# A mixed attention and gated-layer kernel: the products that feed the states are ordered after the scores instead of after the masking

## The chip, the cores and the metric

The kernel runs on one core of a Trainium2 chip. The metric is the device time in microseconds of one execution. The engines are TensorE (PE in the profile; PEld is its weight load), VectorE (DVE), ScalarE (ACT), GpSimd (POOL) and the DMA queues, which SyncE (SP) issues here.

## The reference

A gated linear attention runs over 768 tokens for each of 4 x 8 heads with 48 channels; its outputs for 3072 tokens then go through a gated layer of 384 x 1536 and back.

```python
for t in range(S):
    state = alpha[:, :, t, :, None] * state + np.einsum('bhd,bhe->bhde', k[:, :, t], v[:, :, t])
    y[:, :, t] = np.einsum('bhd,bhde->bhe', q[:, :, t], state)
...
gate = 1.0 / (1.0 + np.exp(-(x @ w_gate)))
val = x @ w_val
return (gate * val @ w_out).astype(np.float32)
```

## The kernel before, in words

**The gated layer.** The 3072 tokens form 6 groups of 512, and the layer's width of 1536 forms 12 blocks of 128, so there are 72 steps (`step`, L570). A step issues nine products of 128x512 into the PSUM bank `pg` (gate, through L208) and nine into `pv` (value). ACT takes the sigmoid of `pg` (`sg`, L581), DVE multiplies `pv` by it in place (L583), ACT rounds the result to `hh` (L585), and DVE writes the rest to `hl` (L586). The products back to 384 outputs (L594) are six with `hh` and three with `hl`. They are issued one step late: those of step s stand behind the gate and value products of step s+1. Each of `pg` and `pv` exists once, so the next `pv` product waits for L586 and the next `pg` product for the sigmoid, or for whatever else has read `pg`.

**The attention.** It is cut into 24 units, each a pair of heads times 512 tokens. Units 0 to 7 work in chunks of 128 tokens (`unit`, L398), units 8 to 23 in chunks of 64 (`late`, L481). In a late unit, in this order of data:

- DVE scales the queries (L501), scans the decays (L353, L355 to L357, L359) and leaves the keys to POOL (L360); PE turns the keys (L372) into `at_117`, and ACT copies them to `kn` (L376).
- PE computes the scores (L512): 16 products into columns 0 to 255 of two banks, `at_118` and `at_119` (`pas` in the code).
- DVE multiplies the scores by the mask into `A` (L517): four instructions, two for each bank.
- PE computes what the unit adds to the states, the "adds" (`adds`, L524, product L528): 16 small products into columns 256 to 447 of the same two banks.
- DVE steps the states through the unit (`states`, L536, L538): eight instructions in a chain, which read the adds out of the banks in turn. POOL multiplies the states by the decays (L543).
- One unit later, PE computes the outputs (L555) into `pg`, ACT and DVE move them to `yt` (L383, L384), and SP sends `yt` to `x` (L392), the gated layer's input of the next group.

Three steps of the gated layer go with each late unit.

**What sets the order.** Nothing is issued as it stands in the code. Each piece is handed to a planner (`Plan`, L45) with an engine, an assumed duration, a key (when it is due) and the names of what it reads and writes. `add` (L59) turns the names into dependences; `order` (L74) then plays the program through with the assumed durations: whenever an engine is free, the ready piece with the smallest key begins, and the pieces are issued in the order of these beginnings. The names are the planner's own: a name such as `at_118`'s stands for a whole bank unless a mark is added to it. The semaphores that the program really waits for are put in afterwards by the layer below, from the buffers that the issued instructions touch and from their order; it is not told of the planner's names.

In a late unit the keys are `A` (scores) = y + 0.50, `Y` (adds) = y + 0.51, `S` (states) = y + 0.55, `mask` = y + 0.6. So the adds are due ahead of the masks, but cannot begin in the plan until what they depend on is done.

Of the kernel before, what the change touches and what calls it, by code (L numbers as in the profile page):

```python
# [18 lines left out]
B, H, S, D = 4, 8, 768, 48  # L19
# [17 lines left out]
CH, EH = T // C, T // E  # L37
# [174 lines left out]
def chunked(ctx, tc, rows, vc, vh, weights_in, out, const, ident, flags, weights, within):  # L212
# [3 lines left out]
    plan = Plan()  # L216
# [12 lines left out]
    def borrow(tag, *shape):  # L229
        t, at = slots[tag]  # L230
        size = 1
        for x in shape:
            size *= x
        slots[tag][1] = at + size
        name = f"{tag}_{at}"
        held[tag].append(name)
        t = t[:, at:at + size]
        if len(shape) == 2:
            t = t.rearrange("p (a b) -> p a b", b=shape[1])
        elif len(shape) == 3:  # L240
            t = t.rearrange("p (a b c) -> p a b c", b=shape[1], c=shape[2])
        return name, t
# [17 lines left out]
    for _ in range(2):  # L260
        nm, t = borrow("w11", WF // 2, 2)
# [84 lines left out]
    def decays(u, size, t, inn, tin):  # L346

        n, nch = T, T // size
        a0, az, kT = tin[:, 0:nch], tin[:, A_Z:A_K], tin[:, A_K:A_Q]
        over = ["later"] if size == E else []  # L350
        (gn, G), (fn, F), (g0n, G0), (decn, dec) = r_G.next(), r_F.next(), r_G0.next(), r_dec.next()
        G0, dec = G0[:, 0:nch], dec[:, 0:nch]
        plan.add("vector", scan(n), t["G"], lambda: nc.vector.tensor_tensor_scan(  # L353
            out=G[:, ::-1], data0=az[:, n:0:-1], data1=d1g[size], initial=0.0, op0=ALU.mult, op1=ALU.add), [(inn, "a"), *over], [gn], port=True)
        plan.add("vector", 0.12, t["G"], lambda: nc.vector.tensor_tensor(out=G0, in0=G[:, 0:n:size], in1=tiny[:, 0:nch], op=ALU.max), [gn], [g0n], port=True)  # L355
        plan.add("vector", 0.12, t["G"], lambda: nc.vector.reciprocal(out=d1f[:, 0:n:size], in_=G0), [g0n], ["d1f"])
        plan.add("vector", scan(n), t["G"] + 0.01, lambda: nc.vector.tensor_tensor_scan(  # L357
            out=F, data0=az[:, 0:n], data1=d1f, initial=0.0, op0=ALU.mult, op1=ALU.add), ["d1f", (inn, "a")], [fn], port=True)
        plan.add("vector", 0.12, t["dec"], lambda: nc.vector.tensor_tensor(out=dec, in0=a0, in1=G[:, 0:n:size], op=ALU.mult), [gn, (inn, "a")], [decn], port=True)  # L359
        plan.add("gpsimd", pool_(n), t["kt"], lambda: nc.gpsimd.tensor_tensor(out=kT, in0=kT, in1=G, op=ALU.mult), [gn, (inn, "r")], [(inn, "k")])  # L360
        plan.add("gpsimd", 0.15, t["flag"], lambda: nc.gpsimd.tensor_copy(out=starts[:, u, 0:nch], in_=G[:, 0:n:size]), [gn], [("start", u)])
        return fn, F, decn, dec
# [5 lines left out]
    def turn(t, inn, kT, pkn, pk):  # L368

        def turned():  # L370
            for c in range(CH):
                nc.tensor.transpose(out=pk[:, c * P:(c + 1) * P], in_=kT[:, c * P:(c + 1) * P], identity=ident)  # L372

        plan.add("tensor", (0.109 * CH + 0.03, 0.9), t["X"], turned, [(inn, "k")], [pkn])
        knn, kn = r_kn.next()
        plan.add("scalar", act(CH * P), t["kn"], lambda: nc.scalar.copy(  # L376
            out=kn.rearrange("p c d -> p (c d)"), in_=pk[:, 0:CH * P]), [pkn], [knn])
        return knn, kn
# [102 lines left out]
    def late(u, g, p, t):  # L481
# [17 lines left out]
        fn, F, decn, dec = decays(u, E, t, inn, tin)  # L499
# [5 lines left out]
        knn, kn = turn(t, inn, kT, pkn, pk)  # L505
# [22 lines left out]
                    nc.tensor.matmul(out=pas[c % 2][1][R * j:R * j + D, T // 2 + c // 2 * D:T // 2 + (c // 2 + 1) * D],  # L528
                                     lhsT=kn[ro, c // 2, R * j:R * j + D], rhs=v[ro, c // 2, j], start=True, stop=True)

        plan.add("tensor", (0.045 * EH + 0.1, 0.5), t["Y"], adds, [knn, (vn, "v")], [x[0] for x in pas])
        st, sn = sts[p], ("st", p)
        done = EH if u >= EARLY + NP else CH
        plan.add("gpsimd", 0.28, t["G"], lambda: nc.gpsimd.tensor_copy(out=st[:, 0, :], in_=st[:, done, :]), writes=[sn])
# [3 lines left out]
                nc.vector.scalar_tensor_tensor(out=st[:, c + 1, :], in0=st[:, c, :], scalar=dec[:, c:c + 1],  # L538
                                               in1=pas[c % 2][1][:, T // 2 + c // 2 * D:T // 2 + (c // 2 + 1) * D], op0=ALU.mult, op1=ALU.add)

        plan.add("vector", 0.265 * EH, t["S"], states, [decn, *(x[0] for x in pas)], [sn])
        for j in range(2):
            plan.add("gpsimd", pool_(EH * D), t["sd"], lambda j=j: nc.gpsimd.tensor_tensor(  # L543
                out=vs[own[j], j], in0=st[own[j], 0:EH], in1=dec[own[j]].rearrange("p (c o) -> p c o", o=1).broadcast_to([R, EH, D]), op=ALU.mult),
# [74 lines left out]
    def begin(u):  # L619
        g, p = divmod(u, NP)  # L620
        if g == 0:
            z = 2.0 * p - 60.0
            t = dict(load=z - 5, G=z, dec=z + 0.5, kt=z, flag=14.0 + u, q=z + 0.2, X=z, kn=z, Y=z + 0.1, A=z, mask=z + 0.3,
                     S=z + 0.2, sd=z + 0.3, out=z + 0.4, y=z + 0.4, run=1, e_q="gpsimd")
        elif g == 1:
            z = 2.0 + 2.5 * p
            t = dict(load=z - 7, G=z, dec=z + 0.5, kt=z, flag=14.0 + u, q=z + 0.2, X=z, kn=z, Y=z + 0.1, A=z, mask=z + 0.3,
                     S=z + 0.2, sd=z + 0.3, out=last_step(u) + 0.52, y=z + 0.4, run=1, e_q="gpsimd")
        else:
            o = last_step(u)  # L630
            y = o - 3
            t = dict(load=y - 5, G=y - 2.9, dec=y - 2, kt=y - 2.7, flag=y + 1 + 0.5 * p, q=y - 2.0, X=y - 0.50, A=y + 0.50, kn=y - 1,
                     Y=y + 0.51, mask=y + 0.6, S=y + 0.55, sd=y + 0.7, out=o + 0.52, y=o - 99, run=100, e_q="vector")
        return unit(u, g, p, t) if u < EARLY else late(u, g, p, t)
# [13 lines left out]
    for s in range(NG * NF):  # L648
        step(s)
        if s in finished:  # L650
# [7 lines left out]
    every, one, total = sb.tile([P, 1], F32, name="every"), sb.tile([P, 1], F32, name="one"), r_at.next()  # L658
    nc.vector.memset(one, 1.0)
    late, n_units = NG * NF - 4, NG * NP  # L660
    plan.add("scalar", 0.5, late, lambda: nc.scalar.activation(out=starts.rearrange("p u c -> p (u c)"), in_=starts.rearrange("p u c -> p (u c)"),
                                                               func=AF.Abs, accum_out=flags[:, n_units:n_units + 1]),
             [("start", x) for x in range(n_units)], [("flag", n_units)])
# [152 lines left out]
```

## Time and profile before

| what | value |
|---|---|
| device time, 3 runs | 577.41, 577.44, 579.86 us (median 577.44) |
| device time of the profiled execution | 577.62 us |
| its span in the trace | 575.9 us |
| mean granted TensorE clock | 0.988 |
| busy: PE, PEld, DVE, ACT, POOL | 554.9, 438.5, 361.8, 184.1, 101.6 us |

The span runs from the first to the last instruction of the program; 1.7 us of the device time lie around it. Times below are microseconds from the start of the span. A row of the timeline gives start, length, engine, line, operation, what it writes and reads with their shapes, the count of merged instructions, and in brackets the idle time of the engine ahead of it with the releaser. The records of PE overlap, since its products are pipelined: what a run of products costs is the distance from its start to the start of the next run.

### The profile page before, as it was taken

The numbers are of one execution on the slowest core, as the hardware profiler recorded it, in microseconds if no ns is written. First come the engines' busy times: TensorE is split into PE (matmuls) and PEld (weight loads), VectorE is DVE, ScalarE is ACT, GpSimd is POOL, SyncE is SP. The second block draws the span as 40 slices with busy tenths as digits, with TensorE's granted clock in tenths as the row PEclk, the third lists the DMA queues.
The fourth block names the chain that finished last, engine by engine and source line by source line (L and its number), as shares of the span: only waits on it lengthen the run. The fifth ranks groups of instructions, "written<-read, shape, count | busy, mean of one in ns | idle before, by whom it ended". The sixth has DMA issues, their size and how long they took to land.

```text
span 575.9 us, 10284 instructions
## 1 busy us (share of the span) xinstructions
PE 554.9 (96%) x4150; PEld 438.5 (76%) x4150; DVE 361.8 (63%) x648; ACT 184.1 (32%) x331; POOL 101.6 (18%) x133
## 2 busy tenths in 40 slices
PE   7978799999999999999999999999999999999995
PEld 4566577787887887887887887888887888888784
DVE  7898999987586586585586586585595342321221
ACT  2568685532322222321222322222322221212111
POOL 5432220323021121121121121120120010000000
PEclk9979899999999999999999999999999999999998
DMA  8866656524234034134034143033132011100001
GB/s 319 265 222 211 224 169 209 163 71 126 75 90 113 8 103 111 62 106 110 3 111 110 56 111 100 11 112 96 70 111 53 9 28 28 56 0 0 2 1 61
DMA packets 21834, 55.93 MB, mean 97 GB/s; under 512 B 3473, under 2 KB 8593, under 8 KB 21777
## 3 DMA queue, kind: packets, MB, share of 16 engines
q1 hardware_dynamic: 21776, 55.17, 31.5%
q8 instruction: 35, 0.57, 0.4%
q14 instruction: 23, 0.18, 0.1%
HBM read 41.01 MB, written 4.72 MB: 79 GB/s over the span
## 4 chain that ended last, share of the span: by engine, by line
PE 88%; DVE 5%; DMA 3%; ACT 2%; POOL 1%; issue 1%; SPq 0%; DVEq 0%
PE po L594 27%; PE pg L208 25%; PE pv L208 25%; PE pg L555 3%; DMA first_w<-in_w_dram 2%; PE at L528 2%; PE at L512 2%; PE at L372 1%; PE at L424 1%; DVE first_w L323 1%; DVE w L327 1%; DMA x<-yt 1%; PE pg L475 1%; PE pg L471 1%; DVE raw L323 1%
## 5 line engine op out<-in xcount | busy, mean ns | idle before, releaser
L208 PE MATMUL pg<-x,w 128*128 128x512 f32 x648 | 164.7, 398 | 6.8 <-DMA x<-yt 2.5
L208 PE MATMUL pv<-x,w 128*128 128x512 f32 x648 | 160.0, 391 | 0.0
L583 DVE TENSOR_TENSOR pv<-pv,sg 128x512 f32<-128x512 f32 x72 | 50.3, 699 | 160.4 <-PE pv L208 159.3
L208 PEld LDWEIGHTS pg<-x,w 128*128 128x128 f32 x648 | 122.9, 191 | 36.7 <-DMA x<-yt 2.7
L208 PEld LDWEIGHTS pv<-x,w 128*128 128x128 f32 x648 | 121.2, 188 | 26.2 <-DVE hl L586 0.4
L594 PE MATMUL po<-hh,w 128*128 128x512 f32 x432 | 117.0, 404 | 0.0
L581 ACT ACTIVATE sg<-pg 128x512 f32<-128x512 f32 x72 | 43.0, 597 | 206.4 <-PE pg L208 206.3
L594 PEld LDWEIGHTS po<-hh,w 128*128 128x128 f32 x432 | 78.4, 188 | 18.0 <-issue 0.6
L543 POOL TENSOR_TENSOR vs<-st,dec 64x384 f32<-64x384 f32 x32 | 31.2, 974 | 239.8 <-DVE st L538 238.6
L585 ACT CAST hh<-pv 128x512 fp32r<-128x512 f32 x72 | 42.4, 588 | 80.2 <-DVE pv L583 80.2
L586 DVE TENSOR_TENSOR hl<-pv,hh 128x512 fp32r<-128x512 f32 x72 | 49.4, 686 | 24.3 <-ACT hh L585 23.7
L594 PE MATMUL po<-hl,w 128*128 128x512 f32 x216 | 64.0, 403 | 0.0
L594 PEld LDWEIGHTS po<-hl,w 128*128 128x128 f32 x216 | 39.5, 188 | 9.5
L360 POOL TENSOR_TENSOR in<-in,G 128x512 f32<-128x512 f32 x22 | 29.8, 1356 | 67.6 <-DVE G L353 38.7
L501 DVE TENSOR_TENSOR A<-A,F 64x512 f32<-64x512 f32 x32 | 37.4, 1170 | 0.9 <-DMA A<-in_rows_dram 0.4
L538 DVE SCALAR_TENSOR_TENSOR st<-st,dec,at 128x48 f32<-128x48 f32 x128 | 33.7, 264 | 5.3 <-PE at L528 0.3
L353 DVE TENSOR_TENSOR_SCAN G<-in,d1g 128x512 f32<-128x512 f32 x22 | 26.8, 1220 | 2.7 <-DMA in<-in_rows_dram 2.2
L357 DVE TENSOR_TENSOR_SCAN F<-in,d1f 128x512 f32<-128x512 f32 x22 | 27.9, 1266 | 0.5
L517 DVE TENSOR_TENSOR A<-at,mask 64x256 f32<-64x256 f32 x64 | 27.0, 422 | 1.1
L376 ACT COPY kn<-at 128x512 f32<-128x512 f32 x22 | 12.9, 585 | 34.5 <-PE at L372 34.5
L365 ACT ACTIVATE F<-F 128x512 f32<-128x512 f32 x23 | 14.5, 632 | 24.1 <-DVE A L501 20.0
L323 DVE SCALAR_TENSOR_TENSOR raw<-raw 128x576 uint32<-128x576 uint32 (+1 forms) x28 | 21.2, 765 | 0.5 <-ACT raw L320 0.5
(132 smaller groups left out, 413.9 us busy)
## 6 DMA issues: line engine op xcount, KB each, us to landing
in<-in_rows_dram SPq DMA_DIRECT2D x16, 516.5 KB, 4.1
raw<-in_w_dram SPq DMA_DIRECT2D x12, 576.0 KB, 4.6
x<-yt SPq DMA_DIRECT2D x35, 192.0 KB, 3.7
first_w<-in_w_dram SPq DMA_DIRECT2D x10, 576.0 KB, 5.4
out_dram<-raw SPq DMA_DIRECT2D x18, 256.0 KB, 2.4
v<-in_vc_dram SPq DMA_DIRECT2D x22, 192.0 KB, 3.5
A<-in_rows_dram SPq DMA_DIRECT2D x32, 128.0 KB, 3.9
in<-in_rows_dram SPq DMA_DIRECT2D x4, 772.5 KB, 7.1
```

The source lines that it names most:

```text
L208: nc.tensor.matmul(out=dst, lhsT=lhs(a, i), rhs=rhs(b, i), start=(n == 0 and i == 0), stop=(n == len(todo) - 1 and i == NK - 1))
L323: plan.add("vector", 0.07 + n / 860, kk, lambda upper=upper, lower=lower, a=a, x=x, y=y: nc.vector.scalar_tensor_tensor(out=lower, in0=upp ...
L357: plan.add("vector", scan(n), t["G"] + 0.01, lambda: nc.vector.tensor_tensor_scan(out=F, data0=az[:, 0:n], data1=d1f, initial=0.0, op0=ALU ...
L360: plan.add("gpsimd", pool_(n), t["kt"], lambda: nc.gpsimd.tensor_tensor(out=kT, in0=kT, in1=G, op=ALU.mult), [gn, (inn, "r")], [(inn, "k")])
L501: plan.add("vector", vec(T), t["q"], lambda j=j: nc.vector.tensor_tensor(out=A[own[j], j], in0=A[own[j], j], in1=F[own[j]], op=ALU.mult), ...
L538: nc.vector.scalar_tensor_tensor(out=st[:, c + 1, :], in0=st[:, c, :], scalar=dec[:, c:c + 1], in1=pas[c % 2][1][:, T // 2 + c // 2 * D:T ...
L543: plan.add("gpsimd", pool_(EH * D), t["sd"], lambda j=j: nc.gpsimd.tensor_tensor(out=vs[own[j], j], in0=st[own[j], 0:EH], in1=dec[own[j]]. ...
L581: plan.add("scalar", act(T), s - 100, lambda: nc.scalar.activation(out=sg, in_=got["g"][1][:, 0:T], func=AF.Sigmoid), [got["g"][0]], [sgn])
L583: plan.add("vector", vec(T), s - 100, lambda: nc.vector.tensor_tensor(out=pv, in0=pv, in1=sg, op=ALU.mult), [sgn], [pvn])
L585: plan.add("scalar", act(T), s - 100, lambda: nc.scalar.copy(out=hh, in_=pv), [pvn], [hhn])
L586: plan.add("vector", vec(T), s - 100, lambda: nc.vector.tensor_tensor(out=hl, in0=pv, in1=hh, op=ALU.subtract), [pvn, hhn], [hln])
L594: nc.tensor.matmul(out=pso_now[m][1][:, 0:T], lhsT=weights.part("o", b, f)[:, m * P:(m + 1) * P], rhs=h[a][:, 0:T], start=(f == 0 and i == ...
```

## The change

The planner's names for the adds and the states in `late` are changed; no instruction is added, removed or resized.

```diff
-        plan.add("tensor", (0.045 * EH + 0.1, 0.5), t["Y"], adds, [knn, (vn, "v")], [x[0] for x in pas])
+        plan.add("tensor", (0.045 * EH + 0.1, 0.5), t["Y"], adds, [knn, (vn, "v"), *(x[0] for x in pas)], [(x[0], "d") for x in pas])
...
-        plan.add("vector", 0.265 * EH, t["S"], states, [decn, *(x[0] for x in pas)], [sn])
+        plan.add("vector", 0.265 * EH, t["S"], states, [decn, *((x[0], "d") for x in pas)], [sn])
```

Before, the adds wrote the two banks, so in the plan they came after every earlier reader of the banks, the four masks. Now they read the banks, which makes them follow the scores alone, and write a part of its own, `"d"`, which the states read. The masks still read the bank's name.

TensorE at a late unit, before. `pg_120` is the outputs' and the gate's bank, `po` the three banks of the products back, `at_118` and `at_119` those of the scores and adds, `x_111` the layer's input; in brackets are the engines whose semaphores a row waits for.

```order
L555 MATMUL pg_120<-A_87,vs_89 48x64 x14
L594 MATMUL po_122<-hh_114,w_544 128x512 x2
L528 MATMUL at_118<-v_80,kn_84 48x48 [waits DMAHW1_49,DVE_49]
L528 MATMUL at_118<-v_80,kn_84 48x48
L528 MATMUL at_119<-v_80,kn_84 48x48 [waits DVE_49]
L594 MATMUL po_122<-hl_116,w_544 128x512
L208 MATMUL pg_120<-x_111,w_647 128x512 [waits DVE_49]
L208 MATMUL pg_120<-x_111,w_647 128x512 x8
L208 MATMUL pv_121<-x_111,w_647 128x512 x9
```

The same unit now; rows that differ from these by the bank alone are left out in both.

```order
L555 MATMUL pg_120<-A_87,vs_89 48x64 x14
L528 MATMUL at_118<-v_80,kn_84 48x48 [waits DMAHW7_49,DVE_49]
L528 MATMUL at_118<-v_80,kn_84 48x48
L528 MATMUL at_119<-v_80,kn_84 48x48 x2
L594 MATMUL po_122<-hh_114,w_544 128x512 x2
L594 MATMUL po_122<-hl_116,w_544 128x512
L208 MATMUL pv_121<-x_111,w_647 128x512 [waits DVE_49]
L208 MATMUL pv_121<-x_111,w_647 128x512 x8
L208 MATMUL pg_120<-x_111,w_647 128x512 [waits DVE_49]
L208 MATMUL pg_120<-x_111,w_647 128x512 x8
```

The adds moved from between the `hh` and the `hl` products to right behind the outputs, ahead of the `hh` products; they kept one wait for DVE and lost the second; and in the step that follows, the value products changed places with the gate products.

VectorE at a late unit, before. The rows L517 are the masks, L538 the first of eight state steps.

```order
L517 TENSOR_TENSOR A_87<-at_118,mask_104 64x4x64 [waits PE_49]
L517 TENSOR_TENSOR A_87<-at_119,mask_104 64x4x64 [waits PE_49]
L517 TENSOR_TENSOR A_87<-at_118,mask_104 64x4x64
L586 TENSOR_TENSOR hl_116<-pv_121,hh_114 128x512 [waits Activation_49]
L517 TENSOR_TENSOR A_87<-at_119,mask_104 64x4x64
L384 TENSOR_TENSOR yt_85<-pg_120,yt_85 128x512 [waits DMAHW6_49,DMAHW7_49,DMAHW5_49,Activation_49]
L538 SCALAR_TENSOR_TENSOR st_110<-st_110,dec_99,at_118 128x48 [waits PE_49]
L501 TENSOR_TENSOR A_86<-A_86,F_92 64x512 [waits DMAHW2_49]
L583 TENSOR_TENSOR pv_121<-pv_121,sg_112 128x512 [waits PE_49,Activation_49]
L353 SCALAR_TENSOR_TENSOR G_90<-in_78,d1g_102 128x512 [waits DMAHW0_49,Pool_49]
L586 TENSOR_TENSOR hl_116<-pv_121,hh_114 128x512 [waits Activation_49]
L355 TENSOR_TENSOR G_94<-G_90,tiny 128x8 [waits DVE_49]
```

The same unit now, from the third mask on.

```order
L517 TENSOR_TENSOR A_87<-at_118,mask_104 64x4x64
L586 TENSOR_TENSOR hl_116<-pv_121,hh_114 128x512 [waits Activation_49]
L538 SCALAR_TENSOR_TENSOR st_110<-st_110,dec_99,at_118 128x48 [waits PE_49]
L384 TENSOR_TENSOR yt_85<-pg_120,yt_85 128x512 [waits DMAHW6_49,DMAHW7_49,DMAHW0_49,Activation_49]
L517 TENSOR_TENSOR A_87<-at_119,mask_104 64x4x64
L501 TENSOR_TENSOR A_86<-A_86,F_92 64x512 [waits DMAHW2_49]
L353 SCALAR_TENSOR_TENSOR G_91<-in_79,d1g_102 128x512 [waits DMAHW1_49,Pool_49]
L355 TENSOR_TENSOR G_95<-G_91,tiny 128x8 [waits DVE_49]
L583 TENSOR_TENSOR pv_121<-pv_121,sg_112 128x512 [waits Activation_49]
L356 RECIPROCAL d1f<-G_95 128x8 [waits DVE_49]
L357 SCALAR_TENSOR_TENSOR F_93<-in_79,d1f 128x512 [waits DVE_49]
L586 TENSOR_TENSOR hl_115<-pv_121,hh_113 128x512 [waits Activation_49]
```

The states moved ahead of `yt` and of the fourth mask; the first three masks stay ahead of them; and the product L583 with the gate, and the L586 behind it, moved behind the scans of the decays.

This holds for units 9 to 23. In unit 8, the first late one, both masks of `at_119` come after the states, and the adds, which stood behind a later gate product before, stand behind the outputs too. Up to there the order is as before. PE also issues the turn of the keys (L372) of units 10 to 22 ahead of the value products of that step, where it stood behind them, and for units 10 to 20 two of the six `hh` products with it. In the queue of SP the load of `v` (L493) now comes ahead of the unit's transfers of `yt` to `x` (L392), not behind or among them.

## The prediction

> **What bounds the kernel now.** I read the busy time of each engine by windows first, then the timelines of PE and DVE over one late unit.
>
> ```profile
> 120.00:150.00 30.00, 30.00 (x243) 24.15 (x242) 23.31 (x46) 8.58 (x18) 7.99 (x10) 1.00 0.28 78
> 250.00:300.00 50.00, 50.00 (x391) 40.28 (x390) 34.57 (x61) 12.74 (x25) 11.05 (x14) 1.00 0.25 69
> 500.00:540.00 40.00, 40.00 (x175) 32.59 (x174) 8.65 (x13) 7.70 (x13) 0.00 (x0) 1.00 0.03 12
> ```
>
> ```profile
> 132.87 0.69 PE L512 MATMUL at<-A,in 48*64 48x64 f32 x32
> ```
>
> The columns of the first are the window, its length, then PE, PEld, DVE, ACT and POOL busy, and the granted clock. From 120 us on PE is busy in every microsecond, at a clock of 1.00, and every late unit lies there: the first one's scores, the second fence, begin at 132.87. So PE's own queue sets the time: a microsecond in which PE stands still is a microsecond on the end, and only what shortens PE's sequence gains anything. DVE, the next, is busy for 34.57 of 50.
>
> ```profile
> 242.67 0.69 PE L512 MATMUL at<-A,in 48*64 48x64 f32 x32
> 243.30 1.10 PE L555 MATMUL pg<-A,vs 128*48 128x64 f32 x32
> 244.33 1.67 PE L594 MATMUL po<-hh,w 128*128 128x512 f32 x6
> 245.93 0.72 PE L528 MATMUL at<-v,kn 64*48 64x48 f32 x32
> 246.58 0.96 PE L594 MATMUL po<-hl,w 128*128 128x512 f32 x3
> 247.38 2.24 PE L208 MATMUL pg<-x,w 128*128 128x512 f32 x9
> 249.46 2.20 PE L208 MATMUL pv<-x,w 128*128 128x512 f32 x9
> 251.50 1.57 PE L594 MATMUL po<-hh,w 128*128 128x512 f32 x6
> 252.91 0.87 PE L594 MATMUL po<-hl,w 128*128 128x512 f32 x3
> 253.62 2.24 PE L208 MATMUL pg<-x,w 128*128 128x512 f32 x9
> 255.69 2.21 PE L208 MATMUL pv<-x,w 128*128 128x512 f32 x9
> 257.74 0.60 PE L372 MATMUL at<-ident,in 128*128 128x128 f32 x4
> 258.10 1.65 PE L594 MATMUL po<-hh,w 128*128 128x512 f32 x6
> 259.58 0.86 PE L594 MATMUL po<-hl,w 128*128 128x512 f32 x3
> ...
> 264.49 0.69 PE L512 MATMUL at<-A,in 48*64 48x64 f32 x32
> ```
>
> One late unit on PE takes 264.49 - 242.67 = 21.82 us, from start to start without a gap. The stretch that the change rearranges runs from the end of the outputs (244.33) to the next step's products (247.38): `hh` 1.60, adds 0.65, `hl` 0.80, together 3.05 us.
>
> ```profile
> 242.85 0.70 DVE L583 TENSOR_TENSOR pv<-pv,sg 128x512 f32<-128x512 f32 x1 [3.73 <-PE pv L208]
> 243.58 1.29 DVE L517 TENSOR_TENSOR A<-at,mask 64x256 f32<-64x256 f32 x3
> 244.90 0.69 DVE L586 TENSOR_TENSOR hl<-pv,hh 128x512 fp32r<-128x512 f32 x1
> 245.60 0.42 DVE L517 TENSOR_TENSOR A<-at,mask 64x256 f32<-64x256 f32 x1
> 246.06 0.69 DVE L384 TENSOR_TENSOR yt<-pg,yt 128x512 fp32r<-128x512 f32 x1
> 246.67 2.42 DVE L538 SCALAR_TENSOR_TENSOR st<-st,dec,at 128x48 f32<-128x48 f32 x8
> 249.01 2.54 DVE L501 TENSOR_TENSOR A<-A,F 64x512 f32<-64x512 f32 x2
> ...
> 252.50 1.23 DVE L353 TENSOR_TENSOR_SCAN G<-in,d1g 128x512 f32<-128x512 f32 x1
> ...
> 255.44 1.23 DVE L357 TENSOR_TENSOR_SCAN F<-in,d1f 128x512 f32<-128x512 f32 x1
> ```
>
> The masks cannot begin at the scores' end (243.30), since the product L583 stands ahead of them and waits for `pv`: they begin at 243.58, the third ends at 243.58 + 1.29 = 244.87, the fourth at 246.02. PE pays little for this now: the adds begin at 245.93, after 1.60 us of `hh` products that cover the masks.
>
> **The wait that stays.** The change frees the adds from the masks in the plan alone. In the order the adds' first row still waits for DVE. Its bank, `at_118`, is read by the first and the third mask; the second wait, for the fourth mask, is gone because that mask now stands behind the states. So the adds wait for the third mask, and what covered it, the `hh` products, now stands behind them. Queued behind the waiting adds are all products of the gated layer.
>
> The Trainium skill's page "PSUM — Partial Sum Buffer", section "PSUM bank collisions raise a hardware error", says that two engines on one bank and 32-partition quadrant at once are an error even at disjoint columns, and that the guard goes by bank and quadrant. By that rule the masks and the adds exclude each other whatever the planner's names say. The order agrees, since the wait is there; no run here shows a collision.
>
> How long PE stands, from the delay between DVE's end and PE's start, and what the adds cost where nothing holds them:
>
> ```profile
> 66.21 0.68 DVE L384 TENSOR_TENSOR yt<-pg,yt 128x512 fp32r<-128x512 f32 x1
> ...
> 66.95 0.78 PE L208 MATMUL pg<-x,w 128*128 128x512 f32 x1 [2.43 <-DVE yt L384]
> ```
>
> ```profile
> 137.59 2.23 PE L208 MATMUL pg<-x,w 128*128 128x512 f32 x9
> 139.75 0.57 PE L528 MATMUL at<-v,kn 64*48 64x48 f32 x32
> 140.25 2.34 PE L208 MATMUL pv<-x,w 128*128 128x512 f32 x9
> 142.43 0.86 PE L594 MATMUL po<-hh,w 128*128 128x512 f32 x3
> ```
>
> - Added: PE starts 66.95 - 66.89 = 0.06 us after DVE ends, so the adds begin at 244.87 + 0.06 = 244.93 instead of 244.33: 0.60 us of standing in each unit.
> - Adds: in unit 8 they take 140.25 - 139.75 = 0.50, against 0.65 in later units, where the fourth mask (to 246.02) ends only after they have begun. That wait goes. I take 0.50; the upper end is 0.65.
> - Removed: changes between large and small products. `hh` products behind small ones and ahead of large ones take 259.58 - 258.10 = 1.48, `hl` behind `hh` take 253.62 - 252.91 = 0.71, against 1.60 and 0.80.
>
> New stretch: 0.60 + 0.50 + 1.48 + 0.71 = 3.29 us against 3.05, so +0.24 us a unit, in units 9 to 23: 15 x 0.24 = 3.6 us. With 0.65 for the adds it is 0.39, 5.9 us in all.
>
> Unit 8 is different: there only two masks, not three, stand ahead of the adds, so I expect no standing. Its adds leave the middle of the gate and value products, which now take 2.16 and 2.18 where elsewhere they take 2.08 (247.38 to 249.46) and 2.04 (249.46 to 251.50): -0.2 us.
>
> The value products swapped with the gate products, and the turn ahead of them, are the same products; I cost them at nothing, if what they wait for comes in time. In times of the unit above, PE then has: adds 244.93, `hh` 245.43, `hl` 246.91, value 247.62, gate 249.66, `hh` 251.74, `hl` 253.15, gate 253.86, turn 255.93 (0.36), two `hh` from 256.29, value at about 256.84. The waits to check:
> - The gate products at 249.66 wait for `yt` (L384), now behind the states. The states begin when DVE is free of L586 (245.59) and end at 248.02; `yt` ends at 248.72. Margin 0.9.
> - The value products at 256.84 wait for L586 of the step before, now behind both scans. The fourth mask ends at 249.15, L501 at 251.70, L353 at 252.95, then L355, L583, L357 and L586 (0.16, 0.70, 1.23, 0.69), with 0.4 for a reciprocal and gaps: 256.1. Margin 0.7.
> - `yt` is 248.72 - 246.75 = 2.0 us later, and so is `x`, which the next group needs after units 11, 15 and 19:
>
> ```profile
> 225.21 1.18 SPq L392 DMA_DIRECT2D x<-yt  x2
> ...
> 231.80 1.55 PE L208 MATMUL pg<-x,w 128*128 128x512 f32 x6
> ```
>
> ```profile
> x<-yt SPq DMA_DIRECT2D x35, 192.0 KB, 3.7
> ```
>
> The second transfer begins at 225.8 and lands by about 229.5, 2.3 us ahead of the products. The products come 0.2 later, so 0.5 is left. A landing slower by 0.8 would cost 0.3 three times, 1 us.
>
> Sum: 3.6 - 0.2 = +3.4 us on the profiled execution's 577.62 us, 581.0. The median of the runs, 577.44, is 0.2 lower, so I predict **580.8 us**, 0.6% slower. A measurement of this kernel can tell about 0.5%, 2.9 us, from no change.
>
> **The rivals.**
>
> *The wait is as harmless as the diff says* (faster). If the third mask ended before 244.33, PE would go straight on from the outputs: 0.50 + 1.48 + 0.71 = 2.69 against 3.05, -0.36 a unit, 15 x -0.36 - 0.2 = -5.6, 571.8 us. It decides at one point: whether the third mask is 0.6 us earlier. Against it: L583, which the masks stand behind, still waits for `pv`, as the 3.73 us of idle time ahead of it show. Chance 0.06.
>
> *Standing and saving cancel* (577.4). For this the standing has to be 0.36, a third mask 0.24 earlier, or the saving larger. Half of the saving is a sum of small distances, and +3.4 is only 0.5 above what can be told, so 0.22 for all that ends within 0.5%.
>
> *A second wait, at the value products.* DVE now does L355 between the scan and the product with the gate, and POOL's work on the keys starts with the end of the same scan.
>
> ```profile
> L501 DVE TENSOR_TENSOR A<-A,F x32: 661/1215/1303, 124.8 to 446.7; 64x512 f32<-64x512 f32 x32
> ```
>
> ```profile
> L355 DVE TENSOR_TENSOR G<-G,tiny x18: 152/943/1046, 95.2 to 428.7; 128x8 f32<-128x8 f32 x16, 128x4 f32<-128x4 f32 x2
> ```
>
> ```profile
> 253.86 1.28 POOL L360 TENSOR_TENSOR in<-in,G 128x512 f32<-128x512 f32 x1 [2.23 <-issue]
> ```
>
> Both rows (shortest, median and longest in ns) show two lengths, and the long one is met where POOL runs, as at L360. If POOL is first after the scan, L355 ends 1.4 us after 252.95 instead of 0.2, L586 ends at 257.3, and the value products wait 0.5 us, in units 9 to 22: 14 x 0.5 = 7, 588 us. Against it: POOL began 0.13 us after the scan's end (253.73), and L355 follows on DVE's own queue; L501 may also be the short one. The Trainium skill's page "SBUF — State Buffer", section "Who interferes with whom", says that a DVE instruction with two SBUF inputs contends with GpSimd's reads and that issue order decides who blocks. By that rule DVE, the earlier, would win and this rival fall; the two lengths agree with the rule. Chance 0.13.
>
> **How the numbers follow.** The forecast with its own range (580.3 to 583.2, the adds at 0.65) has 0.54, and 0.05 goes to late `x` on top of it (about 582); with the second wait (0.13) slower is 0.72. Within 0.5% is 0.22, faster 0.06. Leaving out the faster case and the second wait leaves out 0.19, so the range runs from 577.2 to 583.6.
>
> **What would show it.** In the profile after: PE idle or waiting for DVE L517 ahead of L528, some 0.5 to 0.6 us in 15 units; L528 straight behind L555, with `hh` products 0.5 after it; a unit of 22.06 us instead of 21.82; PE below 100% in windows from 150 us. Wrong would be: no wait there (faster), a wait at `pv` for L586 (slower than my range), or a unit of 21.82.

## The result, and the profile after

| | before | after |
|---|---|---|
| median of the runs, first set | 579.58 us (577.41 to 580.42, 6 runs) | 583.33 us (582.45 to 585.26, 6 runs) |
| median of the runs, second set | 579.38 us (577.14 to 580.52, 11 runs) | 582.94 us (581.84 to 584.52, 6 runs) |
| profiled execution: time, span | 577.62, 575.9 us | 582.92, 580.9 us |
| DVE busy in it | 361.8 us | 341.8 us |
| start to start of two late units | 21.82 us | 22.11 us |

The changed kernel is slower: ratio 1.0077, 95% interval [1.006, 1.0095], and 1.0072 [1.005, 1.0093] in the second set. The ratios follow the means of the runs more than the medians: the means are 579.05 and 583.46 us in the first set (+4.4) and 578.93 and 583.01 in the second (+4.1). The median of 583.33 is 2.5 us above the predicted 580.8. It lies inside the range of 577.2 to 583.6 and 0.1 above the forecast's own range of 580.3 to 583.2; the sections below show where the 2.5 us come from.

PE's wait after the change, from the list of waits (engine, line, the engine waited for; us in total, times, longest):

```profile
PE at L528 <- DVE A L517: 7.9, 15, 0.5
```

The row is new, fifteen waits of 0.5 us, the adds for the third mask, and from 100 us on it is the only one that the list has. The list counts from the modelled end of the last product ahead; from run to run of products, as below, PE stands a little longer.

The late unit that the prediction used, on PE after the change (start, us, engine, line; in brackets the idle time ahead and its releaser):

```profile
244.33 0.69 PE L512 MATMUL at<-A,in 48*64 48x64 f32 x32
244.95 1.10 PE L555 MATMUL pg<-A,vs 128*48 128x64 f32 x32
246.58 0.57 PE L528 MATMUL at<-v,kn 64*48 64x48 f32 x32 [0.53 <-DVE A L517]
247.08 1.67 PE L594 MATMUL po<-hh,w 128*128 128x512 f32 x6
248.59 0.86 PE L594 MATMUL po<-hl,w 128*128 128x512 f32 x3
249.29 2.24 PE L208 MATMUL pv<-x,w 128*128 128x512 f32 x9
251.37 2.20 PE L208 MATMUL pg<-x,w 128*128 128x512 f32 x9
...
257.61 0.60 PE L372 MATMUL at<-ident,in 128*128 128x128 f32 x4
...
258.51 2.23 PE L208 MATMUL pv<-x,w 128*128 128x512 f32 x9
...
...
262.23 2.24 PE L208 MATMUL pg<-x,w 128*128 128x512 f32 x9
...
266.44 0.69 PE L512 MATMUL at<-A,in 48*64 48x64 f32 x32
```

And DVE's part of it:

```profile
245.24 1.29 DVE L517 TENSOR_TENSOR A<-at,mask 64x256 f32<-64x256 f32 x3
...
249.54 0.68 DVE L384 TENSOR_TENSOR yt<-pg,yt 128x512 fp32r<-128x512 f32 x1
```

The outputs take 1.03 us (before: 243.30 to 244.33), so they end at 244.95 + 1.03 = 245.98. The third mask ends at 245.24 + 1.29 = 246.53 and the adds begin at 246.58: PE stands 0.60. Then adds 0.50, `hh` 1.51 and `hl` 0.70, and the step's products begin at 249.29. From 245.98 that is 3.31 us, against 3.05 before. The unit takes 266.44 - 244.33 = 22.11, which is 0.29 more, so 0.26 of it are in this stretch.

Where the two executions part, by the starts of the scores in unit 8 (before: 132.87, in the prediction), unit 9 and unit 23. Before:

```profile
155.41 0.69 PE L512 MATMUL at<-A,in 48*64 48x64 f32 x32
460.82 0.69 PE L512 MATMUL at<-A,in 48*64 48x64 f32 x32
```

After:

```profile
133.57 0.69 PE L512 MATMUL at<-A,in 48*64 48x64 f32 x32
155.88 0.69 PE L512 MATMUL at<-A,in 48*64 48x64 f32 x32
465.43 0.70 PE L512 MATMUL at<-A,in 48*64 48x64 f32 x32
```

Unit 8 takes 22.31 instead of 22.54 (-0.23). The fourteen units 9 to 22 take 309.55 instead of 305.41 (+4.14, 0.296 each). Ahead of unit 8 lie +0.70, where the order is the same in both. With about 0.25 in unit 23, which has the stretch but no turn of keys behind it, the change itself makes -0.23 + 4.14 + 0.25 = +4.2 us.

### The profile page after: what moved, and what is told of

The parts are those of the page before. It is cut to its first block, busy times and chain, and to the rows that moved or that the text cites. A ratio compares the mean times of both kernels' runs of the same rounds, so it can differ in the third digit from the quotient of the medians.

```text
span 580.9 us, 10268 instructions
## 1 busy us (share of the span) xinstructions
PE 552.2 (95%) x4150; PEld 437.8 (75%) x4150; DVE 341.8 (59%) x648; ACT 183.9 (32%) x331; POOL 101.8 (18%) x133
## 4 chain that ended last, share of the span: by engine, by line
PE 81%; DVE 10%; DMA 4%; ACT 1%; issue 1%; SPq 0%; POOL 0%; DVEq 0%
PE po L594 25%; PE pg L208 24%; PE pv L208 24%; DVE A L517 3%; DMA raw<-in_w_dram 3%; DVE pv L583 2%; PE at L528 2%; PE at L372 1%; DVE w L327 1%; DVE raw L323 1%; DVE first_w L323 1%; DMA x<-yt 1%; PE at L424 1%; PE pg L475 1%; DMA in<-in_rows_dram 1%
## 5 line engine op out<-in xcount | busy, mean ns | idle before, releaser
L583 DVE TENSOR_TENSOR pv<-pv,sg 128x512 f32<-128x512 f32 x72 | 50.3, 699 | 184.2 <-PE pv L208 174.5
L594 PE MATMUL po<-hh,w 128*128 128x512 f32 x432 | 118.8, 404 | 0.0
L585 ACT CAST hh<-pv 128x512 fp32r<-128x512 f32 x72 | 42.3, 587 | 117.9 <-DVE pv L583 117.8
L543 POOL TENSOR_TENSOR vs<-st,dec 64x384 f32<-64x384 f32 x32 | 26.4, 826 | 248.8 <-DVE st L538 247.6
L594 PE MATMUL po<-hl,w 128*128 128x512 f32 x216 | 62.6, 397 | 0.0
L586 DVE TENSOR_TENSOR hl<-pv,hh 128x512 fp32r<-128x512 f32 x72 | 49.3, 685 | 20.9 <-ACT hh L585 20.4
L594 PEld LDWEIGHTS po<-hl,w 128*128 128x128 f32 x216 | 40.7, 188 | 10.1
L538 DVE SCALAR_TENSOR_TENSOR st<-st,dec,at 128x48 f32<-128x48 f32 x128 | 33.9, 265 | 5.5 <-DVE st L538 0.5
L517 DVE TENSOR_TENSOR A<-at,mask 64x256 f32<-64x256 f32 x64 | 27.0, 422 | 1.4
L501 DVE TENSOR_TENSOR A<-A,F 64x512 f32<-64x512 f32 x32 | 25.8, 807 | 2.3 <-DMA A<-in_rows_dram 1.3
L555 PE MATMUL pg<-A,vs 128*48 128x64 f32 (+1 forms) x512 | 17.6, 221 | 0.0
```

The costliest lines, as they stand in the source:

```text
L517: plan.add("vector", vec(T // 2), t["mask"], lambda pa=pa, j=j, i=i: nc.vector.tensor_tensor(out=A[other[j], j].rearrange("p (c i t) -> p ...
L583: plan.add("vector", vec(T), s - 100, lambda: nc.vector.tensor_tensor(out=pv, in0=pv, in1=sg, op=ALU.mult), [sgn], [pvn])
L585: plan.add("scalar", act(T), s - 100, lambda: nc.scalar.copy(out=hh, in_=pv), [pvn], [hhn])
L586: plan.add("vector", vec(T), s - 100, lambda: nc.vector.tensor_tensor(out=hl, in0=pv, in1=hh, op=ALU.subtract), [pvn, hhn], [hln])
L594: nc.tensor.matmul(out=pso_now[m][1][:, 0:T], lhsT=weights.part("o", b, f)[:, m * P:(m + 1) * P], rhs=h[a][:, 0:T], start=(f == 0 and i == ...
```

## The experiments

The theory: PE stands for the third mask, and the cheaper joints between large and small products give back a part. The rivals: the place behind the outputs costs this by itself; the loss comes from what DVE does later (`yt`, scans, L586); the early 0.7 us belong to the change. Each ratio is that of a kernel's runs to those of the kernel before, on one chip.

**The adds' move alone.** In the order that the planner gives for the kernel before, only the late adds are moved, behind the outputs and the third mask; the queues of all engines but PE stay as they were.

```
-        for n in self.order():
+        for n in moved(self.parts, self.order()):
...
+def moved(parts, seq):
...
+        if outs:
+            seq.insert(max(masks[2], outs[-1]) + 1, seq.pop(at))
```

> The kernel before, with one move in TensorE's queue: in units 9 to 23 the adds (L528) stand behind the outputs (L555) and ahead of the hh products, as in the changed kernel. All else, the queue of DVE among it, stands as before. Theory (PE stands for the third mask, the saving of the smaller joints covers half of it): the stretch from the outputs to the gate products is 3.30 us instead of 3.05, the unit 22.06 to 22.07 us instead of 21.82, the wait for DVE L517 ahead of L528 0.5 to 0.6 us, and the whole 15 x 0.246 = 3.7 us above the kernel before, ratio 1.0064. The remaining 0.05 us a unit of the changed kernel (22.10 to 22.12) then belongs to the products in swapped order. Rival 1 (the move itself costs all of it): a unit of 22.11, ratio 1.0077. Rival 2 (the loss comes from the later states, yt and scans on DVE, which stand here as before): a unit of 21.82 and no difference in time.

Measured: 582.61 us against 579.13, ratio 1.0068 [1.0044, 1.0093]. One unit on PE:

```profile
244.24 0.69 PE L512 MATMUL at<-A,in 48*64 48x64 f32 x32
...
246.50 0.57 PE L528 MATMUL at<-v,kn 64*48 64x48 f32 x32 [0.53 <-DVE A L517]
...
266.32 0.69 PE L512 MATMUL at<-A,in 48*64 48x64 f32 x32
```

The unit takes 266.32 - 244.24 = 22.08 here, and 22.07 on the mean of all late ones; its list of waits has the row quoted above word for word. The theory had 22.06 to 22.07. So the move alone makes 0.255 of the 0.296 us, with DVE's queue as before: later scans or a later `yt` are not the cause. What is left, 0.04 a unit, belongs to the rest of the change; the section on the prediction finds it at the turn of the keys.

**Short masks in the changed kernel.** Most of the masking of the late units is left out: 8 of 64 columns of a chunk are masked.

```
-                    out=A[other[j], j].rearrange("p (c i t) -> p i c t", i=2, t=E)[:, i],
-                    in0=pa[own[i], 0:T // 2].rearrange("p (c t) -> p c t", t=E),
+                    out=A[other[j], j].rearrange("p (c i t) -> p i c t", i=2, t=E)[:, i, :, 0:8],
+                    in0=pa[own[i], 0:T // 2].rearrange("p (c t) -> p c t", t=E)[:, :, 0:8],
...
```

> The changed kernel, whose late masks (L517) work on 8 of the 64 columns of each chunk alone: most of the masking of the late units is left out, and the order of the instructions stays as in the changed kernel. The third mask then ends before the outputs (L555) do. Theory: the adds wait for nothing, the stretch is 0.50 + 1.50 + 0.70 = 2.70 us instead of 3.30, less than the 3.05 of the kernel before, and the unit 21.5 us; 15 x -0.31 and -0.23 in unit 8 make -4.9 us against the kernel before, ratio 0.9915, and -9 against the changed one. Rival 1 (the standing is the cost of the adds behind the outputs, whatever DVE does): the unit stays at 22.1, ratio 1.0075. Rival 2 (another DVE result ends the wait, the product L583): standing of 0.2 to 0.5 us remains, ratio 0.995 to 1.002.

Measured: 574.44 us against 579.13, ratio 0.9921 [0.9895, 0.9946]. DVE and PE in one unit:

```profile
243.52 0.59 DVE L517 TENSOR_TENSOR A<-at,mask 64x32 f32<-64x32 f32 x3
```

```profile
242.61 0.69 PE L512 MATMUL at<-A,in 48*64 48x64 f32 x32
...
244.27 0.57 PE L528 MATMUL at<-v,kn 64*48 64x48 f32 x32
...
246.98 2.24 PE L208 MATMUL pv<-x,w 128*128 128x512 f32 x9
...
264.13 0.69 PE L512 MATMUL at<-A,in 48*64 48x64 f32 x32
```

The third mask now ends at 243.52 + 0.59 = 244.11, ahead of the outputs' end at 244.27, and the adds follow without a gap. The stretch is 246.98 - 244.27 = 2.71, the unit 21.52. That is 0.59 less than in the changed kernel, just the 0.60 of standing. With the same order as the slower kernel this one is faster than the kernel before, so the place behind the outputs costs nothing by itself: the length of three masks decides.

**The same short masks in the kernel before**, the control.

> The kernel before with the same short masks (most of the masking of the late units left out, order as in the kernel before), the control of the run with the short masks. Theory: here the masks cost the adds only the wait for the fourth one, 0.15 us a unit (adds 0.50 instead of 0.65): unit 21.67 us, 15 x -0.15 = -2.2 us, ratio 0.996. Rival (shorter masks free DVE and make the whole kernel faster by themselves): a unit as short as with the changed order, 21.5, ratio 0.9915.

Measured: 576.53 us against 579.13, ratio 0.9965 [0.9946, 0.9984].

The adds and the `hl` products of one unit, on PE:

```profile
245.66 0.57 PE L528 MATMUL at<-v,kn 64*48 64x48 f32 x32
246.16 0.96 PE L594 MATMUL po<-hl,w 128*128 128x512 f32 x3
```

The adds take 246.16 - 245.66 = 0.50 here, and the unit 21.67: the fourth mask did cost the adds 0.15, as the prediction had it. The difference between the two kernels with short masks, 21.67 - 21.52 = 0.15 a unit, is what the new order is worth when no mask stands in its way and neither order pays for one.

**The adds given to the planner ahead of the masks.** Then masks wait for adds. The edit is made in the kernel before, with that kernel's names.

```
         plan.add("tensor", (0.055 * EH + 0.15, 0.5), t["A"], scores, [(inn, "k"), (an, 2), (an, 3)], [x[0] for x in pas])
+        def adds():
...
+        plan.add("tensor", (0.045 * EH + 0.1, 0.5), t["Y"], adds, [knn, (vn, "v")], [x[0] for x in pas])
         for j, (pan, pa) in enumerate(pas):
...
-        def adds():
...
-        plan.add("tensor", (0.045 * EH + 0.1, 0.5), t["Y"], adds, [knn, (vn, "v")], [x[0] for x in pas])
```

> The adds are given to the planner ahead of the masks, so that the masks wait for the adds and not the adds for the masks; the names of the kernel before are kept (the adds write the banks whole). TensorE's queue has the adds behind the outputs as in the changed kernel, DVE's has the states and yt ahead of all four masks. Theory (the loss is the standing for the third mask): no wait for DVE ahead of the adds, stretch 2.70 us, unit 21.5 us, about 15 x -0.31 - 0.23 = -4.9 us against the kernel before, ratio 0.9915. Rival 1 (the masks, now behind the states, push the scans and L586 back until the value products wait, 0.3 to 0.8 us a unit): unit 21.8 to 22.3, ratio 1.000 to 1.012. Rival 2 (the standing is the cost of the place behind the outputs): unit 22.1, ratio 1.0075.

Measured: 574.13 us against 579.13, ratio 0.992 [0.9891, 0.995]. The adds are L519 and the masks L525 here. PE, and then DVE, in one unit:

```profile
242.25 1.10 PE L555 MATMUL pg<-A,vs 128*48 128x64 f32 x32
243.28 0.57 PE L519 MATMUL at<-v,kn 64*48 64x48 f32 x32
```

```profile
243.89 2.43 DVE L538 SCALAR_TENSOR_TENSOR st<-st,dec,at 128x48 f32<-128x48 f32 x8
...
246.95 1.73 DVE L525 TENSOR_TENSOR A<-at,mask 64x256 f32<-64x256 f32 x4
```

The outputs' 1.03 us end at 243.28, where the adds begin. With whole masks the unit is 21.52, as with short ones, since all four now come behind the states. The list of PE's waits has no row from 100 us on, and that of its weight loads (PEld) none for the scans or L586, so nothing waits for the later scans either.

**The rest of the change alone.** In the changed kernel's order only the `hh` products are put back ahead of the adds.

```
...
+        for x in tensor[at + 1:at + 4]:
+            assert kinds[x] == (0, 1)
+            seq.remove(x)
+            seq.insert(seq.index(n), x)
```

> The changed kernel with one move undone: in units 9 to 23 the hh products stand ahead of the adds again, as before the change. DVE's queue (states, yt and the fourth mask in this order), the swapped products and unit 8 stay as the change has them. Theory: no wait for DVE L517 ahead of the adds; adds 0.50 since the fourth mask is behind the states; hh 1.60 and hl 0.80 as before, so the stretch is 2.90 us, 0.15 less than in the kernel before, and 0.035 more goes to the value products within the hh products. But the adds end 1.0 us later beside the scores than the adds of the kernel before would have to for the swapped order: the states, 2.4 us, and yt behind them end 6.9 us after the scores' start, while the gate products behind the value products could begin at 6.6. So PE waits 0.3 to 0.4 us for yt, the unit is 22.0 to 22.1 us, and the whole 3 us above the kernel before, ratio 1.005. Rival (the gate products do not wait): unit 21.70 us, 15 x -0.11 - 0.23 = -1.9 us, ratio 0.997.

Measured: 584.64 us against 579.38, ratio 1.0093 [1.007, 1.0115], more than the 1.005 expected. PE, then DVE, in one unit, and the row for `yt` in the list of the weight loads' waits from 100 us on:

```profile
247.40 1.67 PE L594 MATMUL po<-hh,w 128*128 128x512 f32 x6
...
250.30 2.25 PE L208 MATMUL pv<-x,w 128*128 128x512 f32 x9
252.69 2.33 PE L208 MATMUL pg<-x,w 128*128 128x512 f32 x9
254.86 1.57 PE L594 MATMUL po<-hh,w 128*128 128x512 f32 x6
```

```profile
251.95 0.68 DVE L384 TENSOR_TENSOR yt<-pg,yt 128x512 fp32r<-128x512 f32 x1
```

```profile
PEld pg L208 <- DVE yt L384: 9.1, 15, 0.9
```

The stretch is 250.30 - 247.40 = 2.90, as expected, and `yt` ends at 252.63. The value products need 2.08 (249.29 to 251.37 in the changed kernel), so PE could have begun the gate products at 252.38; they begin at 252.69, 0.06 after `yt`. That wait of 0.31 bears out the theory. The products' row bears no releaser, and the list of their waits has two of these fifteen alone; the list of their weight loads has all fifteen, and a start 0.06 behind DVE's end is the other sign to look for. Not expected: these gate products take 2.17 us, not 2.04, behind the standing. That is most of what a unit (22.19 on the mean, 0.37 more than before) is above the 22.0 to 22.1 expected. So, with DVE's queue as the change leaves it, the swap of gate and value products is free only because the adds come early.

**The adds in one piece with the scores.** They stand ahead of the outputs.

```
-        plan.add("tensor", (0.055 * EH + 0.15, 0.5), t["A"], scores, [(inn, "k"), (an, 2), (an, 3)], [x[0] for x in pas])
+        def adds():
...
+        plan.add("tensor", (0.055 * EH + 0.045 * EH + 0.2, 0.5), t["A"], lambda: (scores(), adds()), [(inn, "k"), (an, 2), (an, 3), knn, (vn, "v")], [x[0] for x in pas])
...
-        plan.add("tensor", (0.045 * EH + 0.1, 0.5), t["Y"], adds, [knn, (vn, "v")], [x[0] for x in pas])
```

> The adds are one piece with the scores, ahead of the masks and of the outputs in TensorE's queue; DVE's has the states ahead of L586 (hl), then yt and the four masks. Theory: no wait ahead of the adds, 0.36 us a unit saved in the stretch as with the adds first; but the states hold DVE from 1.2 to 3.6 us after the scores' start, L586 ends at 4.3, and the hl products, which could begin at 3.6, wait for it 0.6 to 0.7 us. Unit 22.1 to 22.2 us, 16 x 0.34 = 5 us above the kernel before, ratio 1.009. Rival (the earlier the adds, the better, with no new wait): unit 21.5 us, ratio 0.9915.

Measured: 572.12 us against 579.38, ratio 0.9874 [0.9854, 0.9895], the fastest of all. My expectation was wrong, and its rival was nearly right. The adds are L518, the outputs L554, the back products L593, and L586 of the other kernels is L585. PE, then DVE, in one unit, and the row for L585 in the list of the weight loads' waits from 100 us on:

```profile
242.72 0.69 PE L512 MATMUL at<-A,in 48*64 48x64 f32 x32
243.23 0.54 PE L518 MATMUL at<-v,kn 64*48 64x48 f32 x32
243.70 1.10 PE L554 MATMUL pg<-A,vs 128*48 128x64 f32 x32
...
246.24 0.86 PE L593 MATMUL po<-hl,w 128*128 128x512 f32 x3
...
264.09 0.69 PE L512 MATMUL at<-A,in 48*64 48x64 f32 x32
```

```profile
246.15 0.68 DVE L585 TENSOR_TENSOR hl<-pv,hh 128x512 fp32r<-128x512 f32 x1
```

```profile
PEld pv L208 <- DVE hl L585: 3.4, 15, 0.2
```

The `hl` products begin at 246.24, while DVE still makes an `hl` until 246.83. They read the `hl` of the step before, which has a buffer of its own (L280 makes two); I had taken the nearest L586 for theirs. What does wait for it are the weight loads of the value products, which overwrite the `pv` that L585 reads: 0.2 us, fifteen times, and in this unit the products take 2.12 us (246.94 to 249.06), not 2.08. The unit is 264.09 - 242.72 = 21.37. Against the adds behind the outputs it saves 0.15 more, most of it in two joints: the scores take 0.51 instead of 0.63 with the adds behind them, and the adds 0.47 instead of 0.50.

**The changed kernel once more.**

> The changed kernel once more, for the size of the difference. By the units in its first trace the change itself is 4.2 us (-0.23 in unit 8, 15 x 0.29 and a little at the end) and 0.7 us of the first difference lies ahead of unit 8, where both kernels have the same order. Theory: a unit of 22.10 us again, the scores of unit 8 anywhere between 132.9 and 133.6, ratio 1.007. Rival (the early 0.7 us belongs to the change): the scores of unit 8 at 133.5 or later again.

Measured: 582.94 us against 579.38, ratio 1.0072 [1.005, 1.0093]. The scores' start in units 8, 9 and 23:

```profile
132.83 0.69 PE L512 MATMUL at<-A,in 48*64 48x64 f32 x32
155.15 0.69 PE L512 MATMUL at<-A,in 48*64 48x64 f32 x32
464.72 0.69 PE L512 MATMUL at<-A,in 48*64 48x64 f32 x32
```

The units repeat (309.57 us for fourteen, 309.55 in the first profile). The early part does not: unit 8 begins at 132.83 here and at 133.57 in the first profile of the same kernel, before at 132.87, and with before's order there, in the run with the adds' move alone, at 133.40, and in the run with the `hh` products put back at 134.43. So the early 0.7 us are a matter of the execution, not of the change.

## Why the mechanism was right, and which terms of the sum failed

The mechanism held: the adds stand for the third mask, 0.60 us in fifteen units. What failed is the sum, in two terms. The base of 577.44 us was 2.1 us below the median of six runs, and the turn of the keys in its new place, costed at nothing, takes 0.04 us in each of thirteen units; a smaller part is in the stretch. The forecast's own range, 580.3 to 583.2, missed the median by 0.1. That the wider one, to 583.6, held it is partly luck: all that the working names above 583.2, short of a second wait, is a late `x`, and that did not come.

The rows of PE that show the turn's cost: before, the one that ends the run from the value products on (the rows ahead of it are in the prediction):

```profile
260.28 2.24 PE L208 MATMUL pg<-x,w 128*128 128x512 f32 x9
```

After, a later unit in which the turn has moved and the `hh` products have not, and the scores that begin unit 22, behind which the turn has not moved:

```profile
412.42 0.60 PE L372 MATMUL at<-ident,in 128*128 128x128 f32 x4
...
414.93 1.57 PE L594 MATMUL po<-hh,w 128*128 128x512 f32 x6
...
417.04 2.24 PE L208 MATMUL pg<-x,w 128*128 128x512 f32 x9
...
443.37 0.69 PE L512 MATMUL at<-A,in 48*64 48x64 f32 x32
```

- **What bounds the kernel**: right. Late microseconds count on PE alone. DVE was 20 us less busy after the change and the kernel slower.
- **The wait that stays**: right in place, count and size: 15 units, 0.60 us of standing, shown by the short masks to be the masks' length.
- **The adds at 0.50**: right, 0.50 in the profile after; the control with short masks shows that the 0.15 was the fourth mask's.
- **The joints**: `hl` 0.70 as predicted (0.71), `hh` 1.51 instead of 1.48. The stretch was 3.31 where 3.29 stood.
- **Unit 8**: -0.23, predicted -0.2.
- **The value products and the turn, costed at nothing**: this term was mis-sized. Their waits never came, so far right. Before, value products, turn, six `hh` and the `hl` behind them took 260.28 - 255.69 = 4.59; after, turn, two `hh`, value products, four `hh` and the `hl` take 262.23 - 257.61 = 4.62, 0.03 more, and with the gate products ahead it is 0.04 a unit, in all 0.5 us. It is the turn's new place and not the split of the `hh` products: with the six in one piece it is 417.04 - 412.42 = 4.62 as well. And unit 22, where value and gate products are swapped but the turn stands where it stood, takes 465.43 - 443.37 = 22.06, the forecast's own figure.
- **The sum**: +3.4 forecast. By the traces it was +4.2 (0.04 a unit from the turn, 0.02 from the stretch, in fifteen units about 0.8), by the means +4.4 and +4.1, by the medians 583.33 - 579.58 = +3.75 and 582.94 - 579.38 = +3.56. So the sum was 0.2 to 1.0 us short.
- **The base**: the larger part of the 2.5 us, 579.58 - 577.44 = 2.1 by the medians. I put +3.4 on 577.44, the median of three runs, and on a profiled execution of 577.62. Of 18 runs of the kernel before on one chip the median is 579.13, from 576.05 to 581.0; two of the three lay low. From 579.58 the same sum gives 583.0. The range rested on the same base, so its upper end stood nearer than meant, and the case of no change at 577.4 was 2 us low. What makes executions of one kernel differ by up to 5 us stays open; the traces show a part of it, ahead of unit 8.

The margins: `yt` ended at 250.22, 1.15 ahead of the gate products (0.9 predicted). L586 ended at 256.94, 1.57 ahead of the value products, 0.7 predicted, mostly because L501 came out short. DVE's L586 in that unit:

```profile
256.28 0.66 DVE L586 TENSOR_TENSOR hl<-pv,hh 128x512 fp32r<-128x512 f32 x1
```

The rivals: "as harmless as the diff says" fails at its own point, since the third mask ended 0.55 us after the outputs; the short masks show that its arithmetic was right (-0.36 forecast, -0.30 measured a unit with the moved turn). "Standing and saving cancel", a ratio of 1, is outside both intervals. "Late `x`" has one row in the list of waits, from ahead of the late units. "A second wait at the value products" did not come: L355 follows the scan and POOL starts behind it. The two rows of that unit, DVE's and POOL's:

```profile
253.75 0.17 DVE L355 TENSOR_TENSOR G<-G,tiny 128x8 f32<-128x8 f32 x1
```

```profile
253.85 1.30 POOL L360 TENSOR_TENSOR in<-in,G 128x512 f32<-128x512 f32 x1 [2.02 <-PE pg L208]
```

L355, begun 0.10 us ahead of POOL, keeps its short length. The Trainium skill's page "SBUF — State Buffer", section "Who interferes with whom", says that issue order decides who blocks; these two rows agree.

## What to carry to other kernels

When a wait is taken out of a plan, ask which wait the queue still has, and what had covered it: the adds came forward past the very products that hid the masks. Let the short work that feeds a long chain come first (adds ahead of masks saved 1% where adds behind three masks lost 0.7%), and check for each reader which buffer it reads before calling the nearest writer its releaser. A forecast of some tenths of a per cent needs a base from many runs; of three, two may lie at one end, as here. Products that only change places can still cost something at the joints: ask what now stands next to what.

## What was not expected of the hardware

- Two SBUF operands on DVE: L501 fell from a median of 1215 ns (row in the prediction) to 689 in the changed kernel, and stays at 1213 with the adds' move alone, where DVE's queue is as before. What it met is POOL's product of the states with the decays (L543). In the prediction's unit L543 ran from 248.94 to 251.00 and the two L501 from 249.01 to 251.55. In the changed kernel `yt` and the fourth mask come between the states and L501, so that the two begin at 250.71: the first, 1.03 us, still meets L543, which ends at 251.20, and the second, 0.69 us, does not.

L501 after, and POOL's L543 in that unit:

```profile
L501 DVE TENSOR_TENSOR A<-A,F x32: 669/689/1031, 125.5 to 450.8; 64x512 f32<-64x512 f32 x32
```

```profile
249.47 1.73 POOL L543 TENSOR_TENSOR vs<-st,dec 64x384 f32<-64x384 f32 x2 [16.32 <-DVE st L538]
```

- The joint between two kinds of small products has a price of its own: 32 scores take 0.63 us ahead of the outputs and 0.51 ahead of the adds.
- Nine gate products took 2.17 us right behind a standing of 0.31, and 2.04 without it. Their weight loads wait too: they begin at 252.69 with the products, where those of the value products begin 0.23 ahead of theirs. Whether that is the cause was not tested. The adds, behind a standing of 0.60, show no such surcharge (adds 0.50).
